# One ScalarE function for the activation of V and U, three query buffers, and another order of the steps, in a conformer block on one core

## The chip, the cores and the metric

The kernel runs on one core of one Trainium2 chip. The metric is the device time of one execution in microseconds (us), here the median of three runs. A profile of one further execution, taken by the hardware profiler, comes with it: its span (first to last instruction) and what each engine did in it.

## The reference

The input is a chunked attention over four batches, eight heads and 768 positions of 64 values, followed by a gated feed-forward block:

```python
# attention, per chunk of 32 queries: 8 memory keys and 56 keys around the chunk
scores = scale * np.matmul(q_c, k_full.transpose(0, 1, 3, 2))
a = np.exp(scores - max); a = a / (sum + 1e-09)
x = np.matmul(a, v_full)                       # (4, 768, 512)
# feed-forward
h = x @ w_in                                   # (4, 768, 1024)
h = 0.5 * h * (1.0 + np.tanh(c * (h + 0.044715 * h ** 3)))
u, v = (h[..., :d_ff // 2], h[..., d_ff // 2:])
v_n = (v - mu) / np.sqrt(var + 1e-06) * g_ln
v_s = np.einsum('ts,bsd->btd', w_sg, v_n) + b_sg[None, :, None]
return (x + (u * v_s) @ w_out).astype(np.float32)
```

## The kernel before, in words

The work is cut into named steps, and a table, `ORDER` (lines 36 to 95), lists all of them by hand. Each step issues its instructions on its engine where its name stands in the table (a star sends it to its second engine), and each engine runs what it is given in that order. So the table alone sets what stands behind what on TensorE (PE), VectorE (DVE), ScalarE (ACT), GpSimd (POOL) and on the DMA queue of SyncE (SP). All of them go through one helper at line 106, so the profile's rows are told apart by tiles and not by lines.

Attention runs in 24 units `u` of 128 positions, six to a batch. A unit loads queries and keys (`k`, into one of two `qk` tiles) and values (`v`), makes the scores on PE (`S`, 64 small matmuls in the trace, into the PSUM tile `s`, of which there is one), takes the row maximum (`mx`) and the difference (`sb`) on DVE, the exponential (`ex`) on ACT, the sum, its reciprocal and the scaling (`sm`, `sr`, `nm`), turns the result round (for the first ten units on PE with `T` and a copy `p` to the tile `pt`, later on DVE with `yt` and four DMAs `E`), and multiplies with the values on PE (`A`, 64 small matmuls, into the tile `av`). `xc`, `xh` and `xl` copy the result out of `av` and split it into a high and a low part in the tile `pair`, since every large product is three float32r products: high by high and the two mixed ones.

The feed-forward block of a batch has the products V (six, of 128 positions by 512 columns), U (eight, of 128 columns by 384 positions), W (eight, the mixing over positions, 18 matmuls each) and O (eight, the output product). Each takes one of four PSUM tiles `mm`. The first three V products of batch 0 are split in column halves, `Va` and `Vb`. The activation of V and U is four steps: Square on ACT (`v1`, `u1`), add-multiply on DVE (`v2`, `u2`), Tanh on ACT (`v3`, `u3`), and add-multiply on DVE (`v4`, `u4`), which gives the PSUM tile back (`gelu_steps`, line 450). The result is twice the activation; the factor is taken out by halving `g_ln` and `b_sg` once (`cbh`, on POOL). V is then normalized (`v5` to `v7`) and split (`v8`, `v9`); W is scaled and shifted (`w1`), gated with U (`w2`) and split (`w3`, `w4`); O is added to x (`o1`) and stored (`out`).

The weights come as float64 words and are made float32 on the chip: for each of eight pieces of `w_in` and four of `w_out` a load `r`, a scaling `d1`, the low word `d2`, its sign `d3`, their join `d4`, the high part `d5` (tile `w_in_hi`) and the low part `d6` (tile `w_in_lo`). Between them, in the first 40 us, stand the first attention units and a few matmuls on an identity (`zz`) that compute nothing.

Of the kernel before, what the change touches and what calls it, by code (L numbers as in the profile page):

```python
# [24 lines left out]
GELU_A = 0.044715  # L25
GELU_C = math.sqrt(2.0 / math.pi)
# [4 lines left out]
N_U = 7  # L31
# [5 lines left out]
zz4 k0 k1 S0 mx0 sb0 ex0 z0 sm0 sr0 nm0* S1 zz1 ri13 ri12 d1i12 d2i13* d1i13 k2 mx1 sb1 T0 S2 ex1 v0  # L37
ri11 k3 d2i12 d3i12 d4i12 sm1 d3i13 d5i12 p0 A0 mx2 sr1 sb2 nm1 d4i13 d6i12 S3 zz2 zz3 k4 ri10 ri01 v1
T1 d2i11* d1i11 xh0 d3i11 d4i11 d5i13 ex2 d6i13 d5i11 xl0 mx3 sm2 sb3 sr2 nm2 zz1 Vb00 T2 S4 ri00 d6i11 d1i10
d2i10* ex3 p1 d2i01* xc0 d3i10 d4i10 A1 d3i01 d5i10 d1i01 d6i10 v2 ri02 cb k5 v3 k6 ri03 Va00 d2i00* xc1  # L40
xh1 d1i00 v100 sm3 sr3 p2* mx4 d3i00 d4i01 xl1* nm3* d4i00 v200 T3 A2 d5i01 xh2 sb4 xl2 d1i02 v300 d2i02* ex4
v400 sm4 v500 sr4 d3i02 vx00 Vb01 Va01 Vb02 xc2 p3 d5i00 v101 d6i01 cbh S5 v201 mx5 d6i00* sb5 A3 nm4* vy00
v600 T4 zz1 xc3 xh3 ex5 v301 d1i03 d2i03* p4* d4i02 z5 v401 sm5 d3i03 v700 v800 xl3 Va02 U001 S6 V03 d4i03
v900* mx6 v501 d5i03 u1001 v102 d5i02 v202 sb6 d6i03 d6i02 k7 v4 g51 g11 g10 g21 k8 g20 g40 v302 u2001 sr5
u3001 ex6 vx01 nm5 vy01 v601 z6 A4 ga10 S7 xh4 ga21 ga51 u4001 mx7 v402 xl4 v701 ga20 v801 gb20* v502 sm6 sr6
gb21* vx02 U002 T5 p5 ga40 xc4 gb10 v901 v103 vy02 nm6* ga11 u1002 v203 u2002 v303 U003 u1003 u3002 sb7 v403
# [12 lines left out]
w3013 xc9 mx15 w4011* w4012 v212 v312 v412 v512 Ea5 k17 v12 V11 ex14 yt12 v111 v211 w4013 O011 xl6 U101 nm13
# [65 lines left out]
def conformer_kernel(ctx, tc, qks, vs, w_in, g_ln, w_sgT, b_sg, w_out, out):  # L125
# [522 lines left out]
```

## Time and profile before

| | us |
|---|---|
| median of 3 runs | 379.19 |
| lowest and highest of them | 378.05, 379.78 |
| the profiled execution, its own time | 380.03 |
| its span | 378.2 |

In the profile an engine's busy time is the union of its instructions. PE is busy for nearly the whole span, DVE for two thirds, ACT and POOL for less than half. The stretch up to some 40 us, in which the weights are prepared and the first units run, is called the ramp below; in what follows it PE has work without a break.

### The profile page before, as it was taken

The numbers are of one execution on the slowest core, as the hardware profiler recorded it, in microseconds if no ns is written. First come the engines' busy times: TensorE is split into PE (matmuls) and PEld (weight loads), VectorE is DVE, ScalarE is ACT, GpSimd is POOL, SyncE is SP. The second block draws the span as 40 slices with busy tenths as digits, with TensorE's granted clock in tenths as the row PEclk, the third lists the DMA queues.
The fourth block names the chain that finished last, engine by engine and source line by source line (L and its number), as shares of the span: only waits on it lengthen the run. The fifth ranks groups of instructions, "written<-read, shape, count | busy, mean of one in ns | idle before, by whom it ended". The sixth has DMA issues, their size and how long they took to land.

```text
span 378.2 us, 11075 instructions
## 1 busy us (share of the span) xinstructions
PE 365.2 (97%) x4804; PEld 342.1 (90%) x4804; DVE 254.5 (67%) x472; ACT 152.4 (40%) x292; POOL 120.7 (32%) x144
## 2 busy tenths in 40 slices
PE   5788999999999999999999999999999999999996
PEld 4677888999998998899999888999999888999995
DVE  2997899987967869764455678766573347744642
ACT  2775797655224255440312254532221255531200
POOL 1435466513131322532302234721023065520210
PEclk9989999999999999999999999999999999999999
DMA  8996776855234524525201453104102300000033
GB/s 305 367 330 258 258 264 188 291 177 169 95 123 147 198 55 149 191 49 188 68 4 45 151 159 122 44 9 153 65 0 95 116 9 0 3 0 2 0 115 116
DMA packets 21072, 48.04 MB, mean 127 GB/s; under 512 B 4000, under 2 KB 13216, under 8 KB 21024
## 3 DMA queue, kind: packets, MB, share of 16 engines
q1 hardware_dynamic: 21024, 47.33, 36.9%
q8 instruction: 38, 0.62, 0.7%
q14 instruction: 10, 0.08, 0.1%
HBM read 37.36 MB, written 6.29 MB: 115 GB/s over the span
## 4 chain that ended last, share of the span: by engine, by line
PE 93%; DVE 3%; ACT 1%; DMA 1%; issue 1%; POOL 0%; DVEq 0%
PE mmd L106 23%; PE mmc L106 21%; PE mma L106 21%; PE mmb L106 16%; PE av L106 7%; PE s L106 4%; DMA qka<-in_qks 1%; DVE mxa L106 0%; DVE eb L106 0%; DVE exc L106 0%; DVE rda L106 0%; DVE ea L106 0%; DVE rdb L106 0%; DVE rdc L106 0%; DVE mc L106 0%
## 5 line engine op out<-in xcount | busy, mean ns | idle before, releaser
L106 DVE SCALAR_TENSOR_TENSOR mmd<-mmd,g_half,b_half 128x384 f32<-128x384 f32 x10 | 6.2, 623 | 16.8 <-PE mmd L106 16.8
L106 PE MATMUL mmc<-w_in_hi,paira 128*128 128x512 f32 (+1 forms) x56 | 14.3, 379 | 0.0
L106 DVE SCALAR_TENSOR_TENSOR mma<-mma,g_half,b_half 128x384 f32<-128x384 f32 x8 | 5.0, 625 | 11.9 <-PE mma L106 11.9
L106 PE MATMUL s<-qkb 64*32 64x64 f32 x768 | 10.9, 238 | 1.9 <-DVE ea L106 1.5
L106 PEld LDWEIGHTS av<-pt,va 64*64 64x64 f32 x512 | 9.2, 145 | 3.6 <-issue 2.4
L106 PEld LDWEIGHTS s<-qkb 64*32 64x32 f32 x768 | 8.9, 112 | 3.9 <-DVE ea L106 1.7
L106 PE MATMUL s<-qka 64*32 64x64 f32 x768 | 10.9, 238 | 1.5 <-DMA qka<-in_qks 1.5
L106 PE MATMUL av<-pt,va 64*64 64x32 f32 x512 | 10.3, 230 | 2.1 <-issue 1.6
L106 DVE STREAM_TRANSPOSE y<-na 128x512 f32<-128x512 f32 x14 | 9.9, 706 | 3.5 <-POOL na L106 2.0
L106 PEld LDWEIGHTS s<-qka 64*32 64x32 f32 x768 | 8.9, 112 | 3.3 <-DMA qka<-in_qks 1.6
L106 PEld LDWEIGHTS mmc<-w_in_hi,paira 128*128 128x128 f32 x56 | 10.0, 198 | 1.6
L106 PEld LDWEIGHTS av<-pt,vb 64*64 64x64 f32 x512 | 8.3, 134 | 3.4 <-issue 2.8
L106 POOL TENSOR_TENSOR pairb<-ue,pairb 128x384 fp32r<-128x384 f32 x3 | 3.1, 1020 | 25.5 <-ACT pairb L106 25.5
L106 PE MATMUL mmc<-w_in_hi,pairb 128*128 128x512 f32 x40 | 11.1, 399 | 0.0
L106 ACT ACTIVATE ga<-ga 128x512 f32<-128x512 f32 x12 | 7.5, 628 | 8.5 <-DVE ga L106 8.5
L106 PE MATMUL mmb<-paira,w_in_hi 128*128 128x384 f32 x56 | 10.9, 337 | 0.0
L106 DVE SCALAR_TENSOR_TENSOR ga<-ga,mmc 128x512 f32<-128x512 f32 x12 | 8.2, 684 | 3.9 <-ACT ga L106 3.9
L106 ACT ACTIVATE ea<-ea 128x512 f32<-128x512 f32 x12 | 7.5, 623 | 8.2 <-DVE ea L106 8.2
L106 PE MATMUL av<-pt,vb 64*64 64x32 f32 x512 | 9.3, 220 | 1.4 <-issue 1.0
L106 PEld LDWEIGHTS av<-pt,vc 64*64 64x64 f32 x512 | 8.6, 138 | 2.1 <-issue 0.7
L106 POOL TENSOR_SCALAR rsa<-mva 128x1 f32<-128x1 f32 x8 | 1.8, 223 | 25.7 <-DVE mva L106 11.6
L106 ACT ACTIVATE gb<-gb 128x512 f32<-128x512 f32 x12 | 7.6, 632 | 5.8 <-DVE gb L106 5.8
(521 smaller groups left out, 1229.9 us busy)
## 6 DMA issues: line engine op xcount, KB each, us to landing
qka<-in_qks SPq DMA_DIRECT2D x12, 640.0 KB, 5.1
qkb<-in_qks SPq DMA_DIRECT2D x12, 640.0 KB, 5.3
va<-in_vs SPq DMA_DIRECT2D x8, 512.0 KB, 5.2
vb<-in_vs SPq DMA_DIRECT2D x8, 512.0 KB, 5.4
vc<-in_vs SPq DMA_DIRECT2D x8, 512.0 KB, 3.9
pt<-y SPq DMA_DIRECT2D x112, 32.0 KB, 1.9
out<-xa SPq DMA_DIRECT2D x12, 192.0 KB, 1.9
out<-xb SPq DMA_DIRECT2D x12, 192.0 KB, 2.5
```

Source lines behind the costliest of these rows:

```text
L106: return self.tc.keep_in_program_order(getattr(self.engine, name)(*args, **kw))
```

## The change

It makes the activation of V and U one ACT instruction, `Gelu_apprx_tanh`, which reads PSUM, writes the result and gives the PSUM tile back; the three steps that followed are gone, and so are the halving of `g_ln` and `b_sg` and the factor of 4 at the variance. The function's table is not the one that holds the exponential: the build puts 28 table loads into ACT's program where there was one. There are three `qk` tiles for two, three `g` tiles for two and nine `u` tiles for seven. `w_in` is held as two halves of 512 columns, so that a V product reads one piece of 512 where it read two of 256; a split V product takes the weights of the first two row blocks first. The table `ORDER` is a new one, with other engines for some steps. The cores of the diff:

```diff
-N_U = 7
+N_U = 9
...
-    qk_t = buffers(2, [P, 1280], F32, "qk")
+    qk_t = buffers(3, [P, 1280], F32, "qk")
...
-    w_in_hl = [const.tile([P, 4, 4, 256], F32R, name=f"w_in_{s}") for s in ("hi", "lo")]
-    gs = Slots(buffers(2, [P, 512], F32, "g"))
+    w_in_hl = [const.tile([P, 2, 4, 512], F32R, name=f"w_in_{s}") for s in ("hi", "lo")]
+    gs = Slots(buffers(3, [P, 512], F32, "g"))
...
-        qk, v = qk_t[u % 2], v_t[u % 3]
+        qk, v = qk_t[u % 3], v_t[u % 3]
...
-        def g1(eng):
-            eng.activation(slots.take(key), ps(), AF.Square)
-        def g2(eng):
-            eng.scalar_tensor_tensor(slots.held[key], slots.held[key], 1.0 / GELU_A, ps(), op0=ALU.add, op1=ALU.mult)
-        def g3(eng):
-            eng.activation(slots.held[key], slots.held[key], AF.Tanh, scale=GELU_C * GELU_A)
-        def g4(eng):
-            eng.scalar_tensor_tensor(slots.held[key], slots.held[key], 1.0, ps(), op0=ALU.add, op1=ALU.mult)
+        def gelu(eng):
+            eng.activation(slots.take(key), mms.held[key][:, 0:width], AF.Gelu_apprx_tanh)
             mms.give(key)
...
-                (lambda a, kt=kt: hl[:, a, kt, sl], lambda c, kt=kt: w_in_hl[c][:, 2:4, kt])
+                (lambda a, kt=kt: hl[:, a, kt, sl], lambda c, kt=kt: w_in_hl[c][:, 1, kt])
...
+            cols = slice(256 * h, 256 * h + 256)
+            k = 0
+            for kts in ((0, 1), (2, 3)):
+                for a, c in ((0, 0), (1, 0), (0, 1)):
+                    for kt in kts:
+                        eng.matmul(ps[:, cols], hl[:, a, kt, sl], w_in_hl[c][:, 1, kt, cols], start=(k == 0), stop=(k == 11))
+                        k += 1
```

What the new table does to the queues is shown at three places.

The first is DVE in the ramp, from the add for the sums of unit 3 (`rda`) to the low part of unit 2's x (the row that writes `paira` from `av`), which the product `Vb02` waits for. `ex` and `m` with a letter are tiles of the weight steps. Before:

```order
L106 TENSOR_REDUCE rda<-eb 128x8
L106 RECIPROCAL rda<-rda 128x8
L106 COPY pt<-mmd 128x4x128
L106 TENSOR_REDUCE mxb<-s 128x8
L106 SCALAR_TENSOR_TENSOR exe<-rawe,exe 128x512
L106 SCALAR_TENSOR_TENSOR mf<-mf,exf 128x512
L106 TENSOR_TENSOR paira<-xa,paira 128x4x128
L106 SCALAR_TENSOR_TENSOR me<-me,exe 128x512
L106 SCALAR_TENSOR_TENSOR ga<-ga,mmc 128x512
L106 TENSOR_TENSOR ea<-s,mxb 128x8x64
L106 TENSOR_TENSOR paira<-av,paira 128x4x128
```

Now:

```order
L93 TENSOR_REDUCE rda<-eb 128x8
L93 RECIPROCAL rda<-rda 128x8
L93 TENSOR_REDUCE mxb<-s 128x8
L93 TENSOR_TENSOR ea<-s,mxb 128x8x64
L93 TENSOR_TENSOR paira<-xa,paira 128x4x128
L93 SCALAR_TENSOR_TENSOR exe<-rawe,exe 128x512
L93 TENSOR_TENSOR paira<-av,paira 128x4x128
L93 BN_STATS sta<-ga 128x6
```

The copy to `pt`, two weight steps (`mf`, `me`) and the add-multiply of the activation no longer stand ahead of that row.

The second is ACT in the ramp, from the high part of unit 2's x (`paira` from `av`) on. `ga` is the activated half product of V, `ea` the exponential of unit 4, `pt` the turned result of unit 3, `xa` from `av` the copy of unit 2's x, which has to be out of `av` before `A3` writes there. Before:

```order
L106 CAST paira<-av 128x4x128
L106 ACTIVATE ma<-rawa 128x512
L106 ACTIVATE ga<-ga 128x512
L106 ACTIVATE exa<-rawa 128x512
L106 ACTIVATE ea<-ea 128x8x64
L106 COPY xa<-av 128x4x128
L106 COPY pt<-mma 128x4x128
L106 CAST w_in_hi<-me 128x512
```

Now:

```order
L93 ACTIVATE exe<-rawe 128x512
L93 CAST paira<-av 128x4x128
L93 ACT_TABLE_LOAD
L93 ACTIVATE ga<-mmd 128x512
L93 ACT_TABLE_LOAD
L93 ACTIVATE ea<-ea 128x8x64
L93 COPY pt<-mma 128x4x128
L93 CAST w_in_hi<-mf 128x2x256
L93 ACTIVATE exb<-rawb 128x512
L93 CAST w_in_hi<-me 128x2x256
L93 COPY xa<-av 128x4x128
```

Two table loads, and two more weight steps, now stand ahead of the copy out of `av`, and the conversion of `rawe` stands ahead of them all.

The third is ACT in the second batch, from the exponential of unit 17 (`eb`) to the activation of the U product `U112` (the first rows of that stretch before). `vh` with a letter is a high part of V, a `u` tile from PSUM the activation of a U product, a `g` tile from PSUM that of a V product. Before:

```order
L106 ACTIVATE eb<-eb 128x8x64
L106 CAST pairb<-xa 128x4x128
L106 CAST vhb<-gb 128x512
L106 CAST vha<-ga 128x512
L106 ACTIVATE gb<-mmc 128x512
L106 ACTIVATE uf<-uf 128x384
L106 ACTIVATE gb<-gb 128x512
L106 ACTIVATE ga<-mma 128x512
L106 ACTIVATE ga<-ga 128x512
```

Now:

```order
L93 ACT_TABLE_LOAD
L93 ACTIVATE eb<-eb 128x8x64
L93 CAST vhe<-gb 128x512
L93 ACT_TABLE_LOAD
L93 ACTIVATE uc<-mmb 128x384
L93 ACT_TABLE_LOAD
L93 ACTIVATE ea<-ea 128x8x64
L93 ACT_TABLE_LOAD
L93 ACTIVATE ua<-mmc 128x384
```

The five rows from `eb` to `ua` that do work have four loads among them, where there was none.

## Rows read from the trace of the kernel before

**Rows 1.** The page's busy times of the engines:

```profile
PE 365.2 (97%) x4804; PEld 342.1 (90%) x4804; DVE 254.5 (67%) x472; ACT 152.4 (40%) x292; POOL 120.7 (32%) x144
```

**Rows 2.** Stretches: start:end, length, busy (count) per engine, PE clock, DMA share, GB/s:

```profile
10.00:15.00 5.00, 3.67 (x120) 3.06 (x124) 4.86 (x10) 3.96 (x8) 2.09 (x2) 1.00 0.96 382
...
23.00:25.00 2.00, 1.00 (x55) 0.89 (x59) 1.97 (x5) 1.56 (x3) 1.49 (x2) 1.00 0.91 309
25.00:27.00 2.00, 2.00 (x27) 1.96 (x26) 2.00 (x4) 1.59 (x3) 0.79 (x1) 0.68 0.83 205
27.00:29.00 2.00, 2.00 (x24) 1.67 (x25) 1.65 (x3) 1.30 (x3) 0.00 (x0) 0.50 0.94 332
...
100.00:200.00 100.00, 100.00 (x1424) 93.66 (x1423) 68.01 (x127) 34.56 (x68) 26.84 (x34) 1.00 0.35 112
```

**Rows 3.** The chain of waits in the ramp: start, length, what:

```profile
9.87 0.69 DVE eb L106
...
32.96 1.40 PE mmd L106 x12
...
36.19 1.55 issue
...
40.26 2.08 PE mma L106 x12
...
46.13 1.06 PE av L106 x64
47.19 0.79 PE s L106 x53
```

**Rows 4.** The timeline of DVE in the ramp, the last row of the first place:

```profile
30.66 0.69 DVE L106 TENSOR_TENSOR paira<-av,paira 128x512 fp32r<-128x512 f32 x1 [0.88 <-ACT paira L106]
```

**Rows 5.** The timeline of PE at the first product U, `U001`:

```profile
40.09 0.86 PE L106 MATMUL mma<-paira,w_in_lo 128*128 128x384 f32 x4
```

**Rows 6.** The chain after the ramp: a V product, and two U products:

```profile
60.11 2.78 PE mmc L106 x12
64.74 2.29 PE mmd L106 x12
67.47 2.09 PE mma L106 x12
```

**Rows 7.** Groups by line and shape, ACT and DVE: busy, mean ns, idle before:

```profile
L106 ACT ACTIVATE gb<-gb 128x512 f32<-128x512 f32 x12 | 7.6, 632 | 5.8 <-DVE gb L106 5.8
L106 ACT ACTIVATE eb<-eb 128x512 f32<-128x512 f32 x12 | 7.5, 627 | 4.1 <-POOL pairb L106 2.5 <-DVE eb L106 1.6
L106 ACT ACTIVATE ga<-mmc 128x512 f32<-128x512 f32 x6 | 3.6, 595 | 8.8 <-PE mmc L106 8.8
L106 ACT ACTIVATE ue<-ue 128x384 f32<-128x384 f32 x6 | 3.1, 524 | 0.7 <-DVE ue L106 0.7
L106 ACT ACTIVATE ua<-mma 128x384 f32<-128x384 f32 x3 | 1.4, 481 | 1.0 <-PE mma L106 1.0
L106 ACT ACT_TABLE_LOAD x1 | 1.3, 1283 | 0.7 <-PEq L636 0.7
L106 DVE SCALAR_TENSOR_TENSOR ga<-ga,mmc 128x512 f32<-128x512 f32 x12 | 8.2, 684 | 3.9 <-ACT ga L106 3.9
L106 DVE SCALAR_TENSOR_TENSOR ua<-ua,mma 128x384 f32<-128x384 f32 x6 | 3.3, 547 | 0.9 <-ACT ua L106 0.8
```

**Rows 8.** Groups by line and shape, POOL:

```profile
L106 POOL TENSOR_SCALAR ga<-ga,mvc,rsc 128x512 f32<-128x512 f32 x4 | 8.4, 2097 | 0.3
L106 POOL TENSOR_SCALAR b_half<-b_half 128x768 f32<-128x768 f32 x1 | 2.2, 2157 | 0.0
```

**Rows 9.** A weight load: its issue (timeline), and KB, us to landing (DMA issues):

```profile
15.18 0.49 SPq L106 DMA_DIRECT2D rawe<-in_w_in  x1
...
rawe<-in_w_in SPq DMA_DIRECT2D x1, 512.0 KB, 8.2
```

**Rows 10.** The waits of PE in the whole span: waited for, us, times, longest:

```profile
PE av L106 <- issue: 2.6, 2, 1.6
```

More of the change, by code (lines that the diff above doesn't have):

```diff
@@ L42 @@
[L42 to L46, printed above, removed]
@@ new lines @@
+d2i11 zz5 v2 xl0 d3i11 sr2 nm2* ri00 mx3 xc0 d5i13 T2 d1i11 sb3 p1 ex3 d4i11 d6i13* Vb00 d2i10 d1i10 d5i11 d3i10
+d4i10 d2i01* ri02 A1 d6i11* g50 g30 p2 d3i01 d5i10 sm3 sr3 k5 S4 xc1 d1i01* mx4 d6i10 sb4 xh1 xl1* A2 nm3*
+d1i00* Va00 ri03 d2i00* d3i00 d1i02* v3 xh2 T3 d1i03* v100 xl2 ex4 v500 d2i02 p3 d4i00 d4i01 d5i01 vx00 d3i02
+vy00 d2i03* d6i01 Vb01 Va01 d5i00 Vb02 d4i02 xc2 S5 mx5 d5i02 sb5 k8 ex5 Va02 A3 g40 xc3 sm4 xh3 z5 d6i00* sr4
+S6 d3i03 U001 xl3* v101 v600 sm5 u1001 d4i03 sr5 nm4* T4 v700* V03 g00 v4 k7 p4 v102 mx6 v6 d5i03 v501 v800 vx01
@@ L235, in weight_steps @@
         step("d4" + tag, joined, vector)
-        step("d5" + tag, lambda eng: eng.copy(hi(), mm()), scalar)
+        step("d5" + tag, lambda eng: eng.copy(hi(), like(mm(), hi())), scalar)
         step("d6" + tag, lower, gpsimd, vector)
@@ L240, in conformer_kernel @@
         half, p = (1, i) if i < 4 else (0, i - 4)
-        quarter, kts = 2 * half + p // 2, slice(2 * (p % 2), 2 * (p % 2) + 2)
+        kts = slice(2 * (p % 2), 2 * (p % 2) + 2)
         weight_steps(
@@ L244, in conformer_kernel @@
             raw_t[i % 6], lambda i=i: m_t[i % 6], ex_t[i % 6],
-            *(lambda s=s, quarter=quarter, kts=kts: w_in_hl[s][:, quarter, kts].rearrange("p k n -> p (k n)")
+            *(lambda s=s, half=half, kts=kts, c=256 * (p // 2): w_in_hl[s][:, half, kts, c:c + 256]
               for s in range(2)),
@@ L280, in load_vecs @@
     def load_vecs(eng):
-        eng.dma_start(g_half, g_ln.rearrange("(k p) -> p k", p=P))
-        eng.dma_start(b_half, b_sg.partition_broadcast(P))
-    def halve_vecs(eng):
-        eng.tensor_scalar_mul(g_half, g_half, 0.5)
-        eng.tensor_scalar_mul(b_half, b_half, 0.5)
+        eng.dma_start(g_all, g_ln.rearrange("(k p) -> p k", p=P))
+        eng.dma_start(b_all, b_sg.partition_broadcast(P))
     step("cb", load_vecs, sync)
-    step("cbh", halve_vecs, gpsimd)
     def x_pair(b, half):
@@ L448, in product, with gelu_step @@
                 k += 1
-    def gelu_steps(names, key, width, slots, last=None):
-        def ps():
-            return mms.held[key][:, 0:width]
-        def g1(eng):
-            eng.activation(slots.take(key), ps(), AF.Square)
-        def g2(eng):
-            eng.scalar_tensor_tensor(slots.held[key], slots.held[key], 1.0 / GELU_A, ps(), op0=ALU.add, op1=ALU.mult)
-        def g3(eng):
-            eng.activation(slots.held[key], slots.held[key], AF.Tanh, scale=GELU_C * GELU_A)
-        def g4(eng):
-            eng.scalar_tensor_tensor(slots.held[key], slots.held[key], 1.0, ps(), op0=ALU.add, op1=ALU.mult)
+    def gelu_step(name, key, width, slots):
+        def gelu(eng):
+            eng.activation(slots.take(key), mms.held[key][:, 0:width], AF.Gelu_apprx_tanh)
             mms.give(key)
-        for name, does, eng in zip(names, (g1, g2, g3, g4), (scalar, vector) * 2):
-            step(name, does, eng)
+        step(name, gelu, scalar)
     def v_steps(b, tt):
@@ L554, in half_steps @@
         step("U" + n, mm_u, tensor)
-        gelu_steps([f"u{i}{n}" for i in range(1, 5)], key, HALF, us)
+        gelu_step("u1" + n, key, HALF, us)
         step("W" + n, mm_w, tensor)
```

121 lines of the change are left out of this document (53 added, 68 removed).

## The prediction
> **What bounds the kernel now.** The page's busy times come first: PE is busy for 365.2 of 378.2 us, DVE for 254.5, ACT for 152.4 [rows 1]. Work that leaves DVE or ACT therefore pays only where PE waits for it. The stretches say where: from 100 to 200 us PE is busy for 100.00 of 100.00 us while DVE has 32 us to spare and ACT 65 [rows 2]. The idle time of PE lies in the ramp. There it is DVE that is full, 4.86 of 5 us between 10 and 15, and the DMA engines too, with a share of 0.96 at 382 GB/s [rows 2]; PE is busy for 1.00 of the 2 us from 23 to 25, and in the 4 us after that its granted clock is 0.68 and 0.50, half being the 1.2 GHz level: it fell right behind the idle time [rows 2]. What this costs is 0.32 x 2 + 0.50 x 2 = 1.64 us of full-rate work. The waits of PE add 2.6 us in two stops inside groups `A`, for which the profile shows no releaser [rows 10]; the longer is 1.55 us at 36.19 [rows 3]. So a change can win what the ramp loses, and can lose wherever it makes PE wait in the full stretch behind it.
>
> **The steps removed in the full stretch: nothing.** DVE loses 48 add-multiplies of 0.684 and 64 of 0.547 us [rows 7], 48 x 0.684 + 64 x 0.547 = 67.8 us, a quarter of its time. ACT loses 24 Square of 0.595 and 24 Tanh of 0.632 for V and 32 each of 0.481 and 0.524 for U [rows 7], 29.4 + 32.2 = 61.6 us. PE covers both; I cost them at nothing. If that cover were gone DVE's 68 us would show, but no row says that it is. A PSUM tile also comes back after one instruction where it took four on two engines; PE waits for no PSUM tile now, so this is worth nothing either.
>
> **What ACT gets instead.** I price the new function like the Square that reads the same PSUM tile, 0.595 and 0.481 us [rows 7]: 24 x 0.595 + 32 x 0.481 = 29.7 us. There are 27 more table loads; the one load in the trace took 1.283 us [rows 7], so 34.6 us. ACT ends at 152.4 - 61.6 + 29.7 + 34.6 = 155 us, no more than before. But loads are latency for what is queued behind them, and the densest place is the third one shown. In the new order ACT has there, from the load ahead of unit 16's exponential to the activation of `U112`, six loads, three exponentials, seven activations, a copy and three high parts: 6 x 1.283 + 3 x 0.627 + 5 x 0.481 + 2 x 0.595 + 0.6 + 3 x 0.62 = 15.6 us (copy and high parts taken like the Square and the Tanh). PE has meanwhile two V, five U, two S and two A: 2 x 2.78 + 5 x 2.08 + 2 x 0.79 + 2 x 1.06 = 19.7 us [rows 3, 6]. So ACT is 4.1 us ahead, and with four PSUM tiles I cost the loads there at nothing. That holds up to a load of 1.283 + 4.1 / 6 = 1.97 us.
>
> The rule that speaks against this change is in the Trainium skill, "ScalarE: Activation LUTs", sections "What ACT_TABLE_LOAD costs" and "Table sets: the hidden batching unit": batch activations by table set, since each switch costs about 2.66 us, a load of 1283 ns and a drain of about 1380 ns. The trace agrees with 1283 ns for the load; it has no load in the middle of work, so no row shows the drain. By that figure six switches take 16.0 us, ACT would need 23.9 us in that stretch, and the sum would be 4.2 us higher there.
>
> **The ramp.** On DVE the row `eb` at 9.87 us [rows 3] and the low part of unit 2's x at 30.66 [rows 4] are 32 instructions apart, so 20.79 / 32 = 0.65 us each, waits included. In the new order they are 29 apart: an add-multiply, the copy to `pt`, two scalings by the sums and three weight steps have left, two low words and two low parts have come. That row would start at 9.87 + 29 x 0.65 = 28.7 us, 2 us earlier. Unit 1's low part is two places ahead, at 27.4, done at 28.1. From there PE has three half products of 1.40 us (`Vb01`, `Va01`, `Vb02`), to 32.3, then `S5` of 0.79 and `Va02` of 1.40, to 34.5 [rows 3].
>
> The next step, `A3`, needs `av` empty, which is ACT's copy at the second place shown. Ahead of it is the conversion of `rawe`. Its load was issued at 15.18 and landed 8.2 us later, at 23.4 [rows 9]. In the queue before, 7.47 MB stand up to and with it; in the new one 8.65 MB (a query load and a value load now go ahead). At 382 GB/s [rows 2] 1.18 MB are 3.1 us: 26.5. From there ACT has eleven instructions: two loads of 1.28 and nine of about 0.6, 8.1 us, so the copy is done at 34.6 and `A3` is held up by 0.1. With `A3` (1.06) and `S6` (0.79) PE is at `U001` at 36.5, where it was at 40.09 [rows 5]. Before, a transposition stood there in place of `S6`; I leave that swap at nothing (at most 0.79 us). So 3.6 us is the best case. The worst is that the low clock (1.64) and the longer stop (1.55) come again in full: 0.4 us. The low clock followed idle time, and PE still waits for DVE between its half products, so I charge half of it, 0.8 us; the stop I do not charge, since it came between `S5` and `A3`, which now have `Va02` between them. **Ramp: -2.8 us** (-3.6 to -0.4).
>
> Some steps change engine: five scalings `d1` go to POOL. No row shows one there; the nearest are 2157 ns for 768 columns by one constant, so 1.44 us for 512, and 2097 ns for 512 by two operands [rows 8]. At either, 7 to 10 us in the ramp's last 25, POOL has room; I cost them at nothing, and name the wait for `w_in_lo` at `U001` as what would be late. The load and the halving of `g_ln` and `b_sg` (2.16 us of POOL, [rows 8]) leave the ramp and were behind PE: nothing.
>
> **The V products.** Per matmul, 256 columns take 1.40 / 12 = 116.7 ns [rows 3], 384 take 2.08 / 12 = 173.3 (a U behind another large product), and 512 in two pieces 2.78 / 12 = 231.7 [rows 6]. The line through the first two gives 230.0 for one piece; the 384-column matmul's excess over its columns at 2.4 GHz (13.3 ns) on top of 213.3 gives 226.7. There are 21 x 12 = 252 such matmuls: 0.4 to 1.3 us. As no row has one piece of 512, I take the middle. **V: -0.8 us** (0 to -1.3).
>
> **Switches on PE.** A large product behind a group S, A or T takes 2.29 us where one behind another large product takes 2.09 [rows 6]. The order before has 27 such switches, the new one 31. **Switches: +0.8 us** (0 to +0.8).
>
> **Sum.** -2.8 - 0.8 + 0.8 = -2.8 us on the profiled execution's 380.03, so 377.2. That execution is 0.84 above the median of 379.19, so the median to expect is **376.4 us**. Half a per cent, 1.9 us, is about what a measurement of this kernel tells from no change: 377.3 and 381.1 are the bounds.
>
> **Rivals.** *No change worth the name* (0.24): the ramp does not shorten because low clock and stop come again: -0.4 - 0.8 + 0.8, 378.8 us. For it speaks that both were there before with the same DMA load, and that the bytes ahead of `rawe` grow; against it that DVE's queue is shorter by three.
>
> *Slower, by the loads* (0.13): ACT has to run dry ahead of a load, so that a switch costs more than the 1.97 us at which the second batch's stretch tips. At twice the row, 2.57 us, that stretch loses 6 x 1.283 - 4.1 = 3.6 us; the third batch has six loads as close together and loses as much; in the ramp two loads ahead of the copy delay `A3` by 2.6. Together 9.8 us: 386.2. For it: no row shows a load between two activations. Against it: ACT is idle in over half of the span, and its only load takes 1.283 us.
>
> *More than forecast* (0.10): the ramp at its best, V at 226.7 ns and the switches hidden: -3.6 - 1.3, 374.3 us.
>
> **How the numbers follow.** The forecast has 0.53. Faster by over 0.5%: 0.46 of it and the 0.10 of the last rival, 0.56. Within: 0.07 of it and 0.21 of the first rival, 0.28. Slower: 0.13 and 0.03 of the first, 0.16. The low end is the last rival with DVE at 0.60 us an instruction, which its rows reach where nothing waits (29 x 0.05 = 1.5): 372.8, put at 372.5. The high end takes two thirds of the price of the slower rival: 376.4 + 6.6 = 383.0.
>
> **What would show it.** Right: `U001` starts at 37 to 38 us; PE without waits behind that; 28 loads of about 1.28 us; DVE at some 190 us and ACT at some 155; V products at 2.72 to 2.76. Wrong in the ramp: `U001` near 40, with a clock near 0.5 in some 4 us before it, or PE waiting for `w_in_lo` from POOL. Wrong behind it: waits of PE for `mm` or `av` on ACT, right behind loads.

## The result: slower by 0.6%, and the profile after

The changed kernel takes 381.04 us (median of 20 runs) where the kernel before, beside it on the same chip, takes 378.62 (20 runs): a ratio of 1.0058, 95% interval 1.0038 to 1.0078. The forecast was 376.4, faster. The ratios here and below, unlike the medians, leave out executions more than 1.5% above the fastest of their kernel (here one, 587.55 us at a granted clock of 0.562). The profiled execution took 379.45 us, near the lowest of the 20 (379.28), with a span of 377.6: it shows the change at its best, and the loss has to be looked for in others too.

The page's busy times, the counterpart of [rows 1]:

```profile
PE 364.2 (96%) x4804; PEld 341.1 (90%) x4804; DVE 203.7 (54%) x369; ACT 156.4 (41%) x257; POOL 122.1 (32%) x139
```

DVE is 50.8 us lighter, ACT 4.0 heavier, and PE is as busy as before: the time is PE's, as it was.

Rows of ACT, DVE and PE from the ramp's timeline (start, length, engine, line, operation and tiles, and in brackets the idle time before it and what ended it), to be laid beside [rows 4, 5]:

```profile
26.95 0.68 ACT L93 ACTIVATE exe<-rawe 128x512 int32<-128x512 uint32 x1 [0.49 <-DMA rawe<-in_w_in]
...
28.11 1.28 ACT L93 ACT_TABLE_LOAD   x1
...
29.41 0.60 ACT L93 ACTIVATE ga<-mmd 128x512 f32<-128x512 f32 x1
...
29.69 0.68 DVE L93 TENSOR_TENSOR paira<-av,paira 128x512 fp32r<-128x512 f32 x1
...
30.03 1.28 ACT L93 ACT_TABLE_LOAD   x1
...
31.32 0.63 ACT L93 ACTIVATE ea<-ea 128x512 f32<-128x512 f32 x1
...
34.28 0.58 ACT L93 COPY xa<-av 128x512 f32<-128x512 f32 x1
```

In its times the ramp went as forecast here: `rawe` is there at 26.95 (26.5 forecast), the low part of x starts at 29.69 on DVE (28.7; 30.66 before), the copy out of `av` is done at 34.28 + 0.58 = 34.86 (34.6), and `U001` starts at 37.64 instead of 40.09. The two table loads start 0.02 us behind the instruction ahead of them, and the next one starts 0.01 to 0.02 us behind their end: a switch takes 1.30 to 1.32 us.

One of these agreements is partly luck. The sum had `rawe` later because more bytes stand ahead of it; here its load was issued later and landed sooner (its issue on SP, and KB and us to landing, to be laid beside [rows 9]):

```profile
20.02 0.43 SPq L93 DMA_DIRECT2D rawe<-in_w_in  x1
...
rawe<-in_w_in SPq DMA_DIRECT2D x1, 512.0 KB, 6.9
```

SP issues in order, and a query load ahead of `rawe` had to wait until 19.17 for the scores that still read its tile.

The groups of ACT (busy, mean ns of one, idle time before), for [rows 7]:

```profile
L93 ACT ACT_TABLE_LOAD x28 | 35.9, 1283 | 2.8 <-DVE eb L93 1.7 <-PEq L611 0.7
...
L93 ACT ACTIVATE ga<-mma 128x512 f32<-128x512 f32 x4 | 2.4, 596 | 2.2 <-PE mma L93 2.2
...
L93 ACT ACTIVATE ub<-mmd 128x384 f32<-128x384 f32 x2 | 1.0, 494 | 0.1
```

The prices were right: 28 loads of 1283 ns, and the new function costs what Square did (596 and 494 ns; 595 and 481 before).

PE's waits (waited for, us, times, longest), for [rows 10], and two pieces of the chain of waits (start, length, what):

```profile
PE s L93 <- DMA qka<-in_qks: 4.8, 1, 4.8
PE av L93 <- ACT xa L93: 1.1, 2, 0.6
PE mma L93 <- POOL na L93: 1.0, 1, 1.0
PE av L93 <- issue: 1.0, 1, 1.0
PE mmb L93 <- POOL na L93: 1.0, 1, 1.0
PE mma L93 <- issue: 0.5, 1, 0.5
PE mmb L93 <- issue: 0.3, 1, 0.3
```
```profile
50.63 2.78 PE mmb L93 x12
...
121.35 4.78 DMA qkc<-in_qks
126.14 4.49 DMA out<-xa
```

Behind `U001` PE now stops three times, where it had no wait before: in `T5` (`mma`, 0.54 up to 48.14, no releaser), at `A10` (0.48 of the 1.1 for `xa`, up to 131.33) and in `W201` (`mmb`, 0.33 up to 252.83, no releaser). The chain shows what `A10` waits for: ACT's copy into `xa` has to wait for the stores out of it, and they landed at 126.14 + 4.49 = 130.6. A V product takes 2.78 us, as in [rows 6].

The two ends of that balance, for the profiled executions of both kernels (start of `U001`; from there to the end of PE's last row):

| | `U001` at | from there to the end |
|---|---|---|
| before | 40.09 | 334.58 |
| after | 37.64 | 336.53 |

The ramp gave 2.45 us in these two profiles, and the rest took 1.95 of them back. The medians differ by 2.4, the other way. So two questions stand: why the rest got longer, and why the usual execution does not even show what is left.

### The profile page after: what moved, and what is told of

Its sections match the earlier page's. It is cut to its first block, busy times and chain, and to the rows that moved or that the text cites. A ratio compares the mean times of both kernels' runs of the same rounds, so it can differ in the third digit from the quotient of the medians.

```text
span 377.6 us, 10924 instructions
## 1 busy us (share of the span) xinstructions
PE 364.2 (96%) x4804; PEld 341.1 (90%) x4804; DVE 203.7 (54%) x369; ACT 156.4 (41%) x257; POOL 122.1 (32%) x139
## 4 chain that ended last, share of the span: by engine, by line
PE 88%; DVE 4%; DMA 4%; SPq 2%; issue 1%; ACT 1%; DVEq 0%; ACTq 0%
PE mmb L93 21%; PE mma L93 19%; PE mmc L93 19%; PE mmd L93 18%; PE av L93 7%; PE s L93 4%; SPq L93 2%; DMA qkc<-in_qks 1%; DMA out<-xa 1%; DMA qka<-in_qks 1%; DVE xa L93 0%; DVE eb L93 0%; DVE exa L93 0%; DVE y L93 0%; ACT xa L93 0%
## 5 line engine op out<-in xcount | busy, mean ns | idle before, releaser
L93 ACT ACT_TABLE_LOAD x28 | 35.9, 1283 | 2.8 <-DVE eb L93 1.7
L93 DVE SCALAR_TENSOR_TENSOR mma<-mma,g_all,b_all 128x384 f32<-128x384 f32 x9 | 5.6, 623 | 15.4 <-PE mma L93 15.3
L93 DVE SCALAR_TENSOR_TENSOR mmc<-mmc,g_all,b_all 128x384 f32<-128x384 f32 x9 | 5.6, 625 | 14.0 <-PE mmc L93 13.9
L93 DVE SCALAR_TENSOR_TENSOR mmb<-mmb,g_all,b_all 128x384 f32<-128x384 f32 x8 | 5.0, 624 | 13.6 <-PE mmb L93 13.6
L93 DVE BATCH_NORM_STATS2 sta<-ga 128x6 f32<-128x512 f32 x6 | 4.2, 692 | 13.5 <-ACT ga L93 13.5
L93 PE MATMUL mmd<-paira,w_in_hi 128*128 128x384 f32 x56 | 10.9, 336 | 0.0
L93 DVE TENSOR_REDUCE mxa<-s 128x8 f32<-128x512 f32 x8 | 5.4, 671 | 8.5 <-PE s L93 8.5
L93 PEld LDWEIGHTS mmd<-paira,w_in_hi 128*128 128x128 f32 x56 | 9.8, 188 | 0.0
L93 ACT COPY xa<-av 128x512 f32<-128x512 f32 x9 | 5.3, 585 | 11.0 <-DMA out<-xa 5.6
L93 ACT ACTIVATE eb<-eb 128x512 f32<-128x512 f32 x12 | 7.6, 632 | 5.3 <-DVE eb L93 5.3
L93 PE MATMUL av<-pt,vc 64*64 64x32 f32 x512 | 9.1, 220 | 0.6 <-ACT xa L93 0.6
```

Of the source, the lines that this page charges most:

```text
L93: return self.tc.keep_in_program_order(getattr(self.engine, name)(*args, **kw))
```

## Experiments

Ratios are against the kernel before on the same chip, with 95% intervals. "Rest" is the time from `U001` to PE's last row, read as in the table above.

### Are the table loads the cause? The change again, without its loads, and alone

`a_again` is the changed kernel unedited. `a_tanh` takes its loads away by another function; the activation itself is left out there (a plain Tanh stands in its place):

```diff
-            eng.activation(slots.take(key), mms.held[key][:, 0:width], AF.Gelu_apprx_tanh)
+            eng.activation(slots.take(key), mms.held[key][:, 0:width], AF.Tanh)
```

`b_gelu` puts the one function into the order and buffers of the kernel before (36 loads, the emptied steps dropped, nothing moved), and `b_tanh` is `b_gelu` with the same edit as `a_tanh`, one load, the activation left out:

```diff
-            eng.activation(slots.take(key), ps(), AF.Square)
+            eng.activation(slots.take(key), ps(), AF.Gelu_apprx_tanh)
...
-        for name, does, eng in zip(names, (g1, g2, g3, g4), (scalar, vector) * 2):
-            step(name, does, eng)
+        step(names[0], g1, scalar)
```

> The changed kernel once more, for a second profile and a second set of times. Both theories expect 380.5 to 381.5 us and 1.004 to 1.008 of the kernel before. Theory Q (what the ramp wins, some 3 us, is given back behind it: by four more switches on PE, 0.8 us, and by waits behind the one DMA queue, in which exchanges, stores and loads of the second batch stand one behind the other and which come out differently from run to run): waits of PE of 0.5 to 4 us in all between 100 and 300 us, at av or s, released by a DMA or by ACT's copy out of av that itself waits for a DMA. Theory L (the table loads hold ACT up): waits of PE behind ACT instructions that follow a table load.

> The changed kernel with Tanh in place of the one activation function, so that one table serves all of ACT and 27 of 28 loads go; the activation itself is left out. Theory Q: ACT 35 us less busy, the time as the changed kernel's within 0.6 us, 380.4 to 381.6. Theory L: 378.5 us or less, 2 to 4 us below the changed kernel.

> The kernel before with the one activation function alone, in its own order (the steps 2 to 4 are struck out, nothing is moved), with 36 table loads. Theory Q: within 1 us of the kernel before, 378 to 379.6, since DVE's 68 us and the loads both lie beside PE's work. Theory L: 381 us or more.

> The kernel before with one activation function, Tanh in place of the right one, so that ACT has one table load for 36; the activation itself is left out. It splits what the single function cost in the old order (0.4%). Theory R: loads cost at most 0.5 us, the rest is the ramp (PE reached U001 1.6 us later in that profile, with stops and low clock): 380.5 to 381.5, as with the loads. Theory L: 379 us, 2 us below it.

Measured: `a_again` 380.98 us, 1.0045 [1.0014, 1.0076]; `a_tanh` 381.9, 1.0054 [1.0021, 1.0087]. Without its 27 loads the changed kernel is no faster; the two intervals together leave the loads at most some 0.4% there. In its order they are hidden as far as this can tell, and the rival that put 9.8 us on them falls. `b_gelu` 381.47, 1.0041 [1.0016, 1.0065]; `b_tanh` 379.06, 0.9994 [0.997, 1.0019]. Both came as theory L had it: in the old order the loads do cost about 0.5%, and taking 56 us off DVE (198.2 in `b_tanh`) brings nothing. Where the loads can cost it, the stretch of the ramp shows (start:end, length, busy (count) of PE, PEld, DVE, ACT, POOL, clock, DMA share, GB/s), first `b_gelu`, then `b_tanh`:

```profile
24.00:42.00 18.00, 14.64 (x313) 13.79 (x306) 10.97 (x21) 15.34 (x24) 5.88 (x8) 0.91 0.81 279
```
```profile
24.00:42.00 18.00, 16.13 (x373) 14.95 (x366) 13.91 (x24) 11.43 (x22) 6.34 (x8) 1.00 0.81 277
```

ACT is busy for 15.34 of 18 us with the loads and 11.43 without, PE does 1.5 us less, and `U001` starts at 41.66 and 38.25; the rests are alike (335.0 and 334.8). These two profiles differ in more than the loads, since a stop and half clock, looked at below, came in that of `b_gelu` alone (mean clocks 0.994 and 0.999). But its four executions at a mean clock of 0.997 or more have a median span of 379.0 us, the eight such of `b_tanh` 377.0. So a cost stays without the low clock, and the ramp is where these two profiles have it.

### Which half of the new order loses?

`h_aramp` runs the steps in the new order up to `U001` and in the old one from there; `h_bramp` the reverse. Both have the one function, with 34 and 30 loads.

> The changed kernel with its own order up to the first U product (U001) and from there the order before (with the one activation function), 34 table loads. Theory R (the rest of the new order is 2 to 2.4 us longer than the rest of the old one, by more switches on PE and stops; the ramp's gain of up to 2.5 us comes in some runs alone, since the clock can fall a second time at 26 us): 378.3 to 379.3, 1.5 to 2.5 us below the changed kernel and within 1 us of the kernel before; from U001 to PE's end 334.5 to 335.3 us, as in the kernel before. Theory L (table loads): with 34 loads 381 us or more.

> The other mixture: the old order (with the one activation function) up to U001, from there the new order, 30 table loads. Theory R: from U001 to PE's end 336 to 338.5 us, and 381 to 383 us in all, the slowest of this row, since it has the longer ramp and the longer rest. Theory L: between the two, about 380.5.

`h_bramp` came as expected: 382.89, 1.0079 [1.0048, 1.011], rest 337.4. `h_aramp` missed: 385.27, 1.012 [1.0079, 1.0162]. Its seam makes a wait of its own (2.12 us of PE for DVE ahead of `A4`), and its ramp has the stops of the next section. The old ramp with the new rest shows that the rest is longer; whether the new ramp gains these two can't tell.

### What are PE's stops without a releaser?

In `a_again` (384.65 us in its profile) they decide the ramp. Its stop in `S4`, and the stretches around it (columns as above):

```profile
26.29 0.64 PE L93 MATMUL s<-qkb 64*32 64x64 f32 x19 [1.65 <-issue]
```
```profile
24.00:26.00 2.00, 0.64 (x48) 0.47 (x45) 2.00 (x4) 1.68 (x3) 1.01 (x1) 1.00 0.78 287
26.00:28.00 2.00, 1.71 (x63) 1.54 (x66) 1.20 (x4) 0.72 (x2) 2.00 (x3) 0.52 1.03 322
28.00:30.00 2.00, 2.00 (x38) 1.94 (x33) 2.00 (x4) 1.13 (x2) 2.00 (x2) 0.50 0.89 282
30.00:32.00 2.00, 2.00 (x11) 2.00 (x11) 0.25 (x1) 1.06 (x2) 1.05 (x1) 0.50 1.00 389
```

PE stops for 1.65 us with 19 of `S4`'s matmuls to go, and right behind it the granted clock is 0.50, the 1.2 GHz level, up to 32 us and beyond. `U001` starts at 41.12, 3.5 us later than in the first profile. That S4 stop is the thing the prediction did not have.

The stops sit at fixed places: counted from the program's first matmul, `A0`'s 17th is number 223, `S4`'s 46th 478, `T5`'s third 987. The order before has its stops at the same counts, in other groups: in `A1` (478), in `A3` with 6 matmuls to go (733), which is the longer stop of [rows 3], and in another execution in `Vb02` (605). Steps of about 127, then. The DMA part of the page has a queue that carries instructions, 38 packets and 0.62 MB, so 16 KB each; PE's 4804 matmuls and 4804 weight loads make 253 for a packet, half of them matmuls. The page's line (packets, MB, share of 16 engines):

```profile
q8 instruction: 38, 0.62, 0.7%
```

**Theory C**: PE comes to the end of a packet's worth, and the next packet is late because the DMA engines are full. Groups `S` and `A` run 64 matmuls in about 1 us, so PE gets there early just where these stand together. Three runs test it.

`a_warm` adds matmuls that compute nothing (planned for a steadier clock); it also moves the count:

```diff
-k0 k1 S0 mx0 sb0 ex0 zz5 ...
+zz4 k0 k1 S0 mx0 sb0 ex0 zz5 ...
...
-... ex2 sm2 T1 zz2 S3 ...
+... ex2 sm2 zz4 T1 zz2 S3 ...
...
-... xh1 xl1* A2 ...
+... xh1 xl1* zz2 A2 ...
```

`a_spread` moves the twelve loads of `w_sg` behind `U001` in the table, with the conversions that follow them. `a_early` moves four of them forward, ahead of a query load that holds SP's queue up until 34 us:

```diff
-... v3 xh2 T3 ... k8 ... A3 g40 xc3 ... V03 g00 ... v502 g51 S7 g20 k10 ...
+... v3 g40 g00 g51 g20 xh2 T3 ... k8 ... A3 xc3 ... V03 ... v502 S7 k10 ...
```

> The changed kernel with 20 more matmuls on the identity in the ramp, where PE stands idle (8 ahead of the first scores, 8 ahead of T1, 4 ahead of A2). If the low clock of the ramp follows from idle PE, theory R expects less of it (at most one stretch of 3.4 us below U001) and U001 at 37.5 to 39 us in the profile, 379 to 380.5 us; and the stop inside S4 moves 16 matmuls back (to the 29th of 64 from the 45th), if it hangs on the count of PE's instructions. Theory L: no change, 381.

> The changed kernel with its twelve loads of w_sg, and the conversions behind them, moved later and spread: none is issued ahead of U001, where five or six were, and the six for the first half of the columns come ahead of the six for the second. TensorE's order stays. Theory C (TensorE's own instructions come late because the loads fill the DMA engines): the DMA share at 41 to 45 us falls from 1.02 to under 0.8, the stops at S4, A0 and T5 fall from 0.5 to 1.7 us to under 0.4 us, no stretch at half clock after 24 us, U001 at 37 to 38.5 us, 335 to 336 us from there to the end: 378.8 to 380.0 us. Theory F (the stops come with the count of matmuls whatever the loads do, and what they cost stays): stops and clock as in the changed kernel, 380.5 to 381.5 us.

> The changed kernel with four loads of w_sg (192 KB each) moved on SyncE's queue from behind the query load that waits until 34 us to directly ahead of it, so that they go out at 26.5 to 29 us and land in the stretch from 32 to 37 us, where the DMA engines are nearly idle; nothing else is edited. Theory C (TensorE's instructions are late where loads fill the DMA engines): DMA share at 33 to 36 us up from 0.3, at 42 to 46 us down from 1.02 to under 0.8, and the stop in T5 (0.4 to 0.5 us in the changed kernel, 1.3 us where the loads were bunched until 50 us) gone or under 0.15 us; 335.5 to 336.3 us from U001 to the end, 0.3 to 1 us off the changed kernel: 380.0 to 380.8 us, 1.001 to 1.004 of before. Theory F (the stop comes with the count of matmuls, whatever the loads do): T5 stops for 0.4 us or more again, 380.8 to 382 us.

`a_warm`, 386.2, 1.0167 [1.0136, 1.0198], missed the 379 to 380.5 us expected, and its extra matmuls answered the question of the count. It has eight idle matmuls ahead of `A0` (`zz4`; each counts as two in the trace), and the stop comes after 8 of `A0`'s 64 matmuls instead of after 16: 56 are left behind it, in the changed kernel 48. Rows of PE, first the changed kernel, then `a_warm`:

```profile
13.59 1.51 PE L93 MATMUL av<-pt,va 64*64 64x32 f32 x48 [0.97 <-issue]
```
```profile
13.67 1.72 PE L92 MATMUL av<-pt,va 64*64 64x32 f32 x56 [1.29 <-issue]
...
49.35 0.43 PE L92 MATMUL s<-qkb 64*32 64x64 f32 x6 [3.28 <-issue]
```
```profile
44.00:46.00 2.00, 2.00 (x124) 1.67 (x123) 1.97 (x4) 1.99 (x3) 1.41 (x4) 1.00 1.05 408
46.00:48.00 2.00, 0.07 (x6) 0.00 (x0) 2.00 (x2) 1.26 (x3) 1.57 (x2) 0.90 0.70 265
48.00:50.00 2.00, 0.65 (x7) 0.48 (x7) 0.88 (x2) 1.99 (x4) 0.29 (x1) 0.50 0.01 4
50.00:52.00 2.00, 2.00 (x7) 2.00 (x7) 2.00 (x6) 0.06 (x1) 1.83 (x4) 0.50 0.63 152
```

With 20 more matmuls ahead, the count that fell into `T5` falls into `S7`, where PE had just run 124 matmuls in 2 us beside a DMA share of 1.05: the stop is 3.28 us, the longest of all, and the clock is 0.50 from 48 us on.

`a_spread`, 384.3, 1.0123 [1.0099, 1.0147], did not spread anything and missed all that theory C expected of it (`S4` still stops for 1.73 us, `A0` for 1.12). SP issues in order, and with the early loads gone it stood at the query load until 36.42; the DMA engines idled (share 0.08 and 0.03 at 32 to 36 us), and everything came in a bunch, share 0.97 to 1.06 from 38 to 52. So its time says nothing for or against the theory, but its stop in `T5` does: it grew from 0.54 to 1.27 us. `a_early` did the opposite. The `T5` row of the changed kernel, that of `a_spread`, and the stretches of the changed kernel and of `a_early`:

```profile
48.14 0.38 PE L93 MATMUL mma<-ident,na 128*128 128x128 f32 x2 [0.54 <-issue]
```
```profile
51.33 0.44 PE L92 MATMUL mma<-ident,na 128*128 128x128 f32 x2 [1.27 <-issue]
```
```profile
46.00:48.00 2.00, 1.60 (x10) 1.43 (x10) 1.18 (x2) 1.97 (x3) 0.57 (x2) 1.00 0.92 260
```
```profile
46.00:48.00 2.00, 2.00 (x130) 1.87 (x123) 1.97 (x4) 1.99 (x4) 1.40 (x4) 1.00 0.17 59
```

In `a_early` the DMA share at 46 to 48 us is 0.17 instead of 0.92 and the stop is gone: PE is busy without a break there, and the rest is 335.8, inside the 335.5 to 336.3 expected. (The share at 42 to 46, which was to fall under 0.8, stayed at 0.96 to 0.98.) Since PE comes to `T5` later in that execution (`U001` at 40.23), these two rows alone do not prove it; the packets below do. The time did not follow: 381.64, 1.0063 [1.0027, 1.0099], above the 380.0 to 380.8 expected, and the ramp of the profiled run has its `S4` stop (1.16 us) and half clock.

The traces also keep when each packet of the instruction queue starts and how long it takes, and that settles what PE waits for. All times in us from the span's start:

| stop | packet starts, takes | PE stops, goes on | from the packet's end to there |
|---|---|---|---|
| `before`, `A3` | 35.27, 1.07 | 36.19, 37.74 | 1.40 |
| changed kernel, `A0` | 11.29, 1.03 | 12.62, 13.59 | 1.27 |
| changed kernel, `T5` | 45.76, 1.07 | 47.60, 48.14 | 1.31 |
| changed kernel, `W201` | 250.62, 0.93 | 252.50, 252.83 | 1.28 |
| `a_again`, `S4` | 23.98, 0.93 | 24.64, 26.29 | 1.38 |
| `a_warm`, `S7` | 46.92, 1.09 | 46.07, 49.35 | 1.34 |

The profile of the DMA queues over 0.1 us shows such a packet by itself (packets, MB, share of 16 engines; 67.1% of 1.6 us are 1.07 us). These are the changed kernel at 45.7 to 45.8 and at 250.6 to 250.7, then `a_warm` at 46.9 to 47.0:

```profile
q8 instruction: 1, 0.02, 67.1%
```
```profile
q8 instruction: 1, 0.02, 58.0%
```
```profile
q8 instruction: 1, 0.02, 68.3%
```

In the 19 traces there are 60 stops without releaser, and each ends 1.19 to 1.61 us behind the end of such a packet; none of the nine counts at which they lie (223, 478, 605, 733, 987, 1113, 1494, 1621 and 3904) is passed sooner than 1.19 us behind its packet. In `a_warm` the packet had not even started when PE stopped. So PE waits for its own instructions.

How the traffic comes in shows at `T5`: it delays the start of the packet. That starts 8.1 to 9.1 us behind `U001` in the six traces of the new order that have the stop (8.0 in `a_tanh`, which just misses it), and 6.1 to 7.2 us behind it in the three with the early loads (`a_early` and two of the next section), which have none. In one of these, `a_loads_stores`, `U001` is at 37.84, near the changed kernel's first profile, so a later arrival of PE is not the reason. But full DMA engines are not needed for a stop, so theory C is only half of it. At `W201` they are idle:

```profile
248.00:250.00 2.00, 2.00 (x86) 1.71 (x92) 0.23 (x2) 1.62 (x3) 0.00 (x0) 1.00 0.00 0
250.00:252.00 2.00, 2.00 (x130) 1.87 (x124) 1.83 (x3) 0.98 (x2) 0.00 (x0) 1.00 0.03 8
```

There PE runs 130 matmuls in 2 us (`A18`, `S23` and `A19` stand close together), and the packet, started at 250.62, takes 0.93 us and 1.28 more until PE goes on.

### The other waits behind the ramp

`a_stores` moves three stores of the first batch ahead of the exchanges on SP's queue, so that `xa` is empty in time for `A10`; `a_both` joins that to `a_spread`, `a_loads_stores` to `a_early`:

```diff
-... v110 out001 xl7* ... S14 mx14 v10 ... O012 out002 vx10 ... v12 out003 out000 k16 ...
+... v110 out001 out003 out000 xl7* ... S14 mx14 out002 v10 ... O012 vx10 ... v12 k16 ...
```

`a_best` is `a_loads_stores` with one more step moved, meant for the stop in `W201`. Here unit 19's product with the values comes behind the exchange that writes the next pair into `pt`, so that this unit's attention is of other data; the amount of work stays:

```diff
-... S23 u1203 v825 v925* xc18 A19 Eb10 v924* v922* W201 W212 ...
+... S23 u1203 v825 v925* xc18 Eb10 v924* v922* W201 A19 W212 ...
```

> The changed kernel with three stores of the first batch moved ahead of the exchanges on the DMA queue, so that ACT's copy out of av for unit 9 (5.6 us behind a store in the profile) finds its tile free sooner. Theory Q: 0.5 to 2 us less than the changed kernel, 379 to 380.5, and the 0.5 us wait of PE at av near 131 us gone. Theory L: as the changed kernel.

> The spread loads of the run before and, as in the run with the stores moved, three stores of the first batch ahead of the exchanges on SyncE's queue. Theory C: 378.4 to 379.6 us, no better than the kernel before by more than the measurement tells apart, no wait of TensorE over 0.3 us around 131 us. Theory F: 380.3 to 381.0 us, as with the stores alone (381.0).

> The run before this one, and with it the two other losses behind the ramp taken away: three stores of the first batch ahead of the exchanges on SyncE's queue, and on TensorE the 64 small matmuls of A19 behind the first W product of the third batch instead of ahead of it. By the count of matmuls the stop at W201's fourth matmul then falls 50 matmuls into A19, 4 us later, and should be gone if it waits for instructions under way. Theory Q (the loss behind U001 is these three waits): no stop over 0.15 us at T5, at W201 or A19, no wait over 0.3 us for av at 131 us; 334.6 to 335.4 us from U001 to the end, as before; 379.0 to 380.0 us, 0.998 to 1.002 of before. Against it: if 336 us or more remain, the longer rest lies in the steps themselves (switches of products, waits for mm banks), and the time stays at 380.5 to 381.5 us.

> The changed kernel with the four loads of w_sg ahead of the query load, as in the run with the early loads, and the three stores ahead of the exchanges; A19 stays where the change has it. Theory Q (the loss behind U001 is mostly the waits in T5 and for av at 131 us): no T5 stop, no wait over 0.3 us at 131 us, 335.0 to 335.7 us from U001 to the end; 380.0 to 381.0 us or 1.002 to 1.005 of before, since the ramp keeps its stops in A0 and S4 and its half clock. A time at or under the kernel before would need a ramp without them, which no theory gives this kernel.

`a_stores`: 381.01, 1.0029 [1.0006, 1.0051], not the 379 to 380.5 of theory Q; the wait at `A10` is gone, but the rest is 336.5 all the same, with 0.90 us in `T5` and 0.60 in `W201`. `a_both` 383.82, 1.0127 [1.0104, 1.0149], is no better than `a_spread` and outside both its theories. `a_best`: 380.7, 1.0032 [1.0004, 1.0059], not the 379 to 380 expected. The row of `W201` in the changed kernel, and in `a_best`:

```profile
252.83 0.33 PE L93 MATMUL mmb<-w_sg_hi,vhd 128*128 128x384 f32 x1 [0.33 <-issue]
```
```profile
253.28 0.68 DVE L92 TENSOR_TENSOR vhc<-gb,vhc 128x512 fp32r<-128x512 f32 x1
254.01 0.44 PE L92 MATMUL mmb<-w_sg_hi,vhc 128*128 128x384 f32 x1 [0.62 <-DVE vhc L92]
```

The stop without releaser is gone from `W201` as the count said, and a data wait has taken its place: `A19` had covered the low part `vhc`, which DVE ends at 253.28 + 0.68. So nothing is won; the rest is 335.9, between the two cases of its expectation. The third, `a_loads_stores`, has neither the `T5` stop nor the `A10` wait, and a rest of 335.7, the upper end of what was expected; its time, 381.46, 1.0047 [1.0023, 1.007], is above the 380 to 381 expected. No version beats the kernel before.

These runs bound what the steps themselves cost. Taking the waits of PE behind `U001` off each rest: 336.5 - 0.54 - 0.48 - 0.33 = 335.2 (changed kernel), 335.8 - 0.49 - 0.25 = 335.0 (`a_early`: `W201`, and `S12` for its query load), 335.7 - 0.19 - 0.47 = 335.0 (`a_loads_stores`, the same two). Before it is 334.6 to 335.1. So of the 2 us by which the rest is longer in the first profile, 1.35 are waits; for the steps 0 to some 0.5 us are left, no more than the rests of the kernel before differ among themselves.

### Which ramp is the usual one?

The forecast was summed on one profile of the kernel before. `b_again`, `b_look1` and `b_look2` are that kernel, unedited; `a_third` is the changed one.

> The kernel before, nothing edited: a second profile of its ramp. If the stops and the half clock of the ramp that its first profile shows (U001 at 40.1 us) are its usual case, they come again, at 379.5 to 380.5 us. If the usual execution, 1 us faster by the median, has a better ramp than the one profiled, U001 starts at 38 to 39.3 us and the low stretch is missing or ends before 24 us, with 334.3 to 335 us from U001 to the end in either case. The ratio is 1 within 0.003.

> The kernel before, nothing edited, one look. Its two profiles so far have a mean granted clock of 0.994 and 0.995, with one stretch of 3.4 us at half clock in the ramp and U001 at 40.1 and 41.0 us, while most of its other executions show 0.999 or 1.0. Theory P (the profile that the prediction was summed on shows a ramp worse than the usual one): an execution at 0.999 or 1.0 has U001 at 38 to 38.8 us, no stretch at half clock after 20 us, 334.5 to 335 us from U001 to the end and a span of 376 to 377.5 us. Against it: U001 at 40 us or later at that clock too, and then 332 to 333 us from there to the end. An execution at 0.995 tells nothing between the two.

> The kernel before once more. Theory P: at a clock of 0.999 or 1.0, U001 at 38 to 38.8 us and 334.5 to 335 us from there to the end; against it: U001 at 40 us or later.

> The changed kernel once more, nothing edited: the run that the next two are compared with on the same chip, and a third look at its ramp. Every theory: 380.5 to 381.5 us, 1.003 to 1.006 of before. The theory that the usual execution loses the ramp's gain to stops and a second stretch at half clock: the profile shows a stop of over 0.5 us with no releaser between 22 and 34 us and a stretch at granted clock 0.5 that begins after 24 us, U001 from 39 to 41.5 us. If what the first profile shows (U001 at 37.6 us, no second stretch) is the usual case, it shows that again.

`b_again`: 379.22, 0.9993 [0.997, 1.0015]; its profile (381.35 us) has a stop of 2.51 us in `A3`, a clock of 0.50 from 38 to 40, `U001` at 40.99. `b_look1` (382.55 us) is the same again. `b_look2` caught the other kind, a mean granted clock of 0.998. Rows of PE in `b_look1` (the `A3` stop and `U001`), then in `b_look2`:

```profile
38.06 0.31 PE L106 MATMUL av<-pt,va 64*64 64x32 f32 x6 [2.63 <-issue]
...
42.00 0.86 PE L106 MATMUL mma<-paira,w_in_lo 128*128 128x384 f32 x4
```
```profile
36.10 0.31 PE L106 MATMUL av<-pt,va 64*64 64x32 f32 x6 [0.29 <-issue]
...
38.47 0.86 PE L106 MATMUL mma<-paira,w_in_lo 128*128 128x384 f32 x4
```

The stop is 0.29 us instead of 2.63, the clock stays at 1.00, and `U001` starts at 38.47. `b_tanh`, whose order is the same, gives 38.25. (The rest of `b_look2`, 336.7, missed the 334.5 to 335 expected: two more stops without releaser, 0.61 in `A8` and 0.92 at `W001`; without them 335.1.) By the clock this is the usual kind: of 109 executions of the kernel before that ran beside the experiments, 64 have a mean clock of 0.997 or more, with a median span of 377.1 us; the other 45 have 378.5. The execution that the prediction read, 378.2 at 0.994, belongs to the 45.

Of 37 executions of the changed kernel (its 20 less one, `a_again`, `a_third`) 8 are at 0.997 or more, with a median span of 378.8; the other 29 have 379.5. (For some of these the low stretch lies at 13 to 20 us, where PE waits anyway, as in the first profile.) `a_third` is a profile at a clock of 1.00 with the ramp as forecast, `U001` at 37.53, and still a span of 378.9, since `A10` waits longer:

```profile
132.50 1.32 PE L93 MATMUL av<-pt,vb 64*64 64x32 f32 x64 [1.32 <-ACT xa L93]
```

Its expectation (a stop and half clock in the ramp) missed: only the stop of 0.95 us in `S4` came. As a timed run it has 382.57, 1.0102 [1.0058, 1.0145], from six runs that reach from 380.03 to 385.6.

## Why the prediction was wrong, by its own steps

- **"Steps removed in the full stretch: nothing"**: right. DVE lost 50.8 us in the page and 56.3 in the old order, and `b_tanh` shows 0.9994 for it. (The page counts overlapping instructions once; added up one by one, DVE's fell by 64.0 in the old order, near the 67.8 of the sum.)
- **The loads at nothing**: right in the new order within some 0.4% (`a_tanh` 1.0054 beside `a_again` 1.0045), and ACT at 156.4 for 155 forecast. The rival "slower, by the loads" had the right sign for the wrong cause. In the old order it would have been right, by the ramp (`b_gelu`). The Trainium skill, "ScalarE: Activation LUTs", section "What ACT_TABLE_LOAD costs", has a switch as a load of 1283 ns and a drain of about 1380 ns. The trace agrees on the load and disagrees on the drain; between two activations it shows 1.30 to 1.32 us in all.
- **"Ramp: -2.8 us"**: this step failed, and twice. As a walk it was good to about 1 us (`U001` at 37.5 to 37.6 where no second fall of the clock comes; 36.5 was the best case). But its other end was one profile, and the 0.84 us by which that stood above the median were carried over as if both kernels had the same loss. The usual execution before has no half clock behind the ramp's middle and `U001` at 38.3 to 38.5 (`b_tanh` and `b_look2`): there was 0.6 to 0.9 us to win, not 2.5. That the first profile of the changed kernel has `U001` inside the 37 to 38 us of the sign "right" is partly luck: of the four traces of the changed kernel whose ramp is unedited two have it (37.64, `a_third` 37.53) and two do not (`a_again` 41.12, `a_stores` 40.29). And of the changed ramp it said "the stop I do not charge", because it no longer stood between `S5` and `A3`. The stop hangs on the count of matmuls and on when the packet of instructions comes; it came in `S4` instead, 1.65 us in `a_again` with half clock behind it. The rival "no change" named this mechanism.
- **The scalings on POOL at nothing**: right. They took 1.52 to 2.04 us in the profile, where 1.44 to 2.1 was taken, and PE has no wait for `w_in_lo` at `U001`.
- **"V: -0.8 us"**: nothing. One piece of 512 columns takes 2.78 us per product as two of 256 did; the end of its range that gains nothing was the value.
- **"Switches: +0.8 us"**: not shown. By the prediction's own count 25 of the 27 and 26 of the 31 stand behind `U001`, so the rests hold one more, 0.2 us by its price; they leave 0 to 0.5 us for all steps together.
- **"PE without waits behind that"**: the second failure. The full stretch was costed at nothing with ACT as the only danger; the moves on SP's queue were not walked past the ramp. They put the stores of `xa` behind exchanges and loads (`A10`: 0.48 in the first profile, 1.54 in `a_again`, 1.32 in `a_third`) and a bunch of `w_sg` loads beside `T5` (0.38 to 0.99 us). The stop in `W201` (0.33 to 0.46 us) came without traffic, where the new order has three groups of small matmuls nearly in a row.

At full clock the parts now come to -0.8 (ramp), 0 (V), 0 to +0.5 (steps) and +1.35 to +2.55 (the waits behind `U001`: 0.54 + 0.48 + 0.33 in the first profile, 0.38 + 1.32 + 0.37 and 0.48 for DVE ahead of `S7` in `a_third`), which is +0.55 to +2.25; the spans there differ by 378.8 - 377.1 = +1.7. The measured ratio, 1.0058, is 2.2 us. Left open: why the packet for `S4` (or `A3`) starts later in one execution than in the next and why the clock falls behind some stops only, for no edit kept the stop in `S4` away without one elsewhere; and what the versions without waits would take with a ramp at full clock, since single edits of under 1 us drown in its spread.

## What to carry to other kernels

Before a gain is summed on a profile, ask from the clock and span of several executions whether the loss that it removes is there in the usual one; what only a part of the executions show is no more than its share of the median. When an order moves steps, walk the DMA queue past every place where the tensor engine comes close to its input, not only to the first: a queue that issues in order moves its stores and loads as a bunch. And many small matmuls in a row run through their own instructions: where several such groups stand together, above all beside a full set of DMA engines, look for a stop that no semaphore explains, and lay it beside the packets of the instruction queue.

## What the runs showed of the hardware that was not expected

- PE stops without a releaser at nine counts of matmuls, 126 to 128 or a multiple of that apart, whatever step stands there; 8 matmuls more ahead move the stop 8 places forward (`a_warm`). Each of the 60 stops (0.19 to 3.28 us) ends 1.19 to 1.61 us behind a 16 KB packet of the instruction queue; a packet itself takes 0.88 to 2.1 us. The longest came beside a DMA share of 1.05 (`S7` in `a_warm`); at shares of 0.00 to 0.03 there were still 0.33 us (`W201`, behind 130 matmuls in 2 us) and 1.15 us (the same count, in `A19`, in `a_warm`).
- Behind some of these stops the granted clock went to 0.50 (the 1.2 GHz level): behind 1.65 us in `S4` it did (`a_again`), behind 0.95 us it did not (`a_third`). The length alone does not tell: in the first profile of the kernel before, the clock fell behind the 1.00 us in `A1` and stayed at 1.00 behind the 1.55 us in `A3`.
- A table load between two activations costs its own 1.28 us and some 0.03 more.
